# Cached GQA decode block on one core: V of the first seven heads loaded by ScalarE's DMA queue

## The chip, the cores and the metric

The kernel runs on one core of one Trainium2 chip. The time is that of one execution on the device, in microseconds. Before the change it is 656.65 us, the median of three runs (656.56 to 656.92).

## The reference

One token goes through an attention block with a KV cache and then through a gated MLP, each behind a LayerNorm and with a residual. Sizes: D = 512, 32 query heads, 8 KV heads (4 query heads share one), 65,536 cached positions, head size 128, F = 1792, all in bf16.

```python
def _A_ref(x, k_cache, v_cache, wq, wo):
    q = (x @ wq) ...                    # 32 heads of 128
    k = jnp.repeat(k_cache, rep, axis=1)
    v = jnp.repeat(v_cache, rep, axis=1)
    scores = jnp.einsum("bhqd,bhkd->bhqk", q, k) * (Dh ** -0.5)
    p = _softmax(scores, axis=-1)
    o = jnp.einsum("bhqk,bhkd->bhqd", p, v)
    return (...o...) @ wo
...
h = x + _A_ref(_layernorm(x), A_k_cache, A_v_cache, A_wq, A_wo)
h2 = h + _B_ref(_layernorm(h), B_w_gate, B_w_up, B_w_down)   # sigmoid(g) * u, then w_down
```

K and V are 134 MB each (8 heads x 65,536 x 128 x 2 bytes) and are read once. With the weights the program reads 282.33 MB.

## The kernel before, in words

**Program.** All instructions are recorded in lists, one for each engine (`Prog.op`, `Prog.dma`), with the names of what they depend on. `Prog.emit` turns the names into semaphore waits. An engine runs its list in order. A DMA is issued by the engine in whose list it stands: that engine waits for what the DMA needs, issues it, and goes on; the data move later. Line numbers in the profile's DMA rows (L339 for K and V, L341 for wq, L358 for wo, L368 and L373 for the B weights, L325 for x) are those of the issuing instruction; the rows call SyncE's issuing SPq and ScalarE's ACTq, and the queues q1 (SyncE's) and q10 (ScalarE's).

**Loads.** Each of the 8 KV heads has a K and a V of 16.8 MB. Each is loaded in two pieces of 8.39 MB (`PIECES`): 128 partitions with 64 KB each, which is 16 chunks of 4 KB (`CH` elements). They go to `ring`, an SBUF buffer of 36 chunks in each partition. K's piece 0 lies in chunks 0 to 15, K's piece 1 in 4 to 19, and both pieces of V in 20 to 35 (`AT`). So K's next piece can come once 12 of the 16 chunks of the last one have been used, and V's next piece once all of the last one has been used. The names: K2.1 is piece 1 of K of head 2. K of head 0 comes in four smaller loads, ahead of everything but wq.

**VectorE.** `dve_block` transposes K chunk by chunk from `ring` into `ktw` (L531), 16 chunks for each piece. After 12 of them a tiny memset (L534) gives the mark F: `F1.0` says that K1.0 has left chunks 4 to 15, `F1.1` the same for K1.1. VectorE also takes the maxima (L538), the transpose of the softmax weights P (L587) and the sums.

**TensorE.** `pe_scores` multiplies the transposed chunks by q (L443, `PS<-ktw`), 4 parts of 8 chunks to a head. The products with V (`pv`, also L443, `PS<-ring,PT_sb`) of head h run during head h+1: those of piece 0 after part 1 of the scores (their end is `PV{h}.1`), those of piece 1 after part 3 (`PV{h}.3`).

**ScalarE.** Each head has its softmax exponentials (L577), the scaling of the output (`head_out`, L618, waits for `PV{h}.3`), a copy (L624), the clearing of the output bank (L504) and the next head's weights (L500).

**Order of the loads.** All but x are issued by SyncE, in one list:

```python
for h in range(1, HKV):
    load("K", h, 0, ["F0.0" if h == 1 else f"F{h - 1}.1"], "ka", f"K{h}.0")
    load("V", h - 1, 0, ["F0.1" if h == 1 else f"PV{h - 2}.3"], "va", f"V{h - 1}.0")
    load("K", h, 1, [f"F{h}.0"], "kb", f"K{h}.1")
    load("V", h - 1, 1, [f"PV{h - 1}.1"], "vb", f"V{h - 1}.1")
```

The list of names in a `load` is what the load waits for. After this loop come V7.0 (after F7.1), wo, V7.1 and the weights of B.

Of the kernel before, what the change touches and what calls it, by code (L numbers as in the profile page):

```python
# [13 lines left out]
HKV = 8  # L14
GS = 4
NQ = 32
DH = 128
D = 512
FF = 1792
# [16 lines left out]
class Prog:  # L36
# [14 lines left out]
    def op(self, eng, fn, deps=(), name=None, to=None, times=1):  # L51
        assert name is None or name not in self.where, name
        self.ops[eng].append(dict(fn=fn, deps=[d for d in deps if d], name=name, dma=None, to=to, times=times, part=self.part.get(eng)))
        if name:
            self.where[name] = (eng, len(self.ops[eng]) - 1)

    def dma(self, eng, fn, sem, deps=(), name=None):
        self.op(eng, fn, deps, name)
        rec = self.dma_sems.setdefault(sem, dict(sem=None, count=0))
        rec["count"] += 16  # L60
        self.ops[eng][-1]["dma"] = (sem, rec["count"])
# [162 lines left out]
def bass_sequential_preLN__gqa_block_cached__glu_gated_glu__decode_kernel(  # L224
# [10 lines left out]
    CH = TC * DH  # L235
    PIECES = ((0, 16), (16, 32))
    RING = 36 * CH
    AT = {"K": (0, 4), "V": (20, 20), "K0": (0, 20), "V7": (0, 20), "wg": 0, "wd": 7}
# [3 lines left out]
    WO = ((0, 28), (28, 4))  # L242
    RW = 4
    WD_SPLIT = [(0, 8), (8, 11), (11, 13), (13, 14)]
    FG = FF // 4

    with ExitStack() as es:
        def sb(name, shape, dt):
            return es.enter_context(nc.sbuf_tensor(name, shape, dt))
# [14 lines left out]
        ring = sb("ring", [128, RING], bf16)  # L264
        ktw = sb("ktw", [128, NKT * CH + WH], bf16)
# [56 lines left out]
        op, dma = P.op, P.dma  # L322
# [3 lines left out]
        W_SPLIT = {"wg": [(0, 4)], "wu": [(0, 4)]}  # L326
        W_AT = {"wg": AT["wg"] * CH, "wu": AT["wg"] * CH + 4 * FF}
        LAST = [(16, 26), (26, 32)]

        def first_chunk(k, h, q):  # L330
            return AT[{("K", 0): "K0", ("V", HKV - 1): "V7"}.get((k, h), k)][q]

        def load(k, h, q, deps, sem, name, cols=None):
            j0, j1 = PIECES[q]
            a, z = cols or (j0, j1)
            cache = A_k_cache if k == "K" else A_v_cache
            rows = cache[0, h, j0 * TC * 128:j1 * TC * 128, :].rearrange("(p t) d -> p (t d)", p=128)
            at = (first_chunk(k, h, q) - j0) * CH
            dma("sp", lambda e: e.dma_start(ring[:, at + a * CH:at + z * CH], rows[:, (a - j0) * CH:(z - j0) * CH]), sem, deps, name)  # L339

        dma("sp", lambda e: e.dma_start(ktw[:, 0:NKT * CH].rearrange("p (k n) -> p k n", k=4),  # L341
                                        A_wq.rearrange("(p k) n -> p k n", p=128)), "r0", (), "wq")
        for q in range(2):
            for i in range(2):
                j0 = 16 * q + 8 * i
                load("K", 0, q, (), f"r{2 * q + i + 1}", f"K0.{q}{'ab'[i]}", (j0, j0 + 8))
        for h in range(1, HKV):
            load("K", h, 0, ["F0.0" if h == 1 else f"F{h - 1}.1"], "ka", f"K{h}.0")
            load("V", h - 1, 0, ["F0.1" if h == 1 else f"PV{h - 2}.3"], "va", f"V{h - 1}.0")
            load("K", h, 1, [f"F{h}.0"], "kb", f"K{h}.1")  # L350
            load("V", h - 1, 1, [f"PV{h - 1}.1"], "vb", f"V{h - 1}.1")
        h = HKV - 1
        load("V", h, 0, [f"F{h}.1"], "va", f"V{h}.0")
        def load_wo(i, deps):
            j0, nj = WO[i]
            src = A_wo[j0 * DH:(j0 + nj) * DH, :].rearrange("(p r) n -> p (r n)", r=nj)
            dst = ktw[:, j0 * D:(j0 + nj) * D]
            dma("sp", lambda e: e.dma_start(dst, src), f"wo{i}", deps, f"wo{i}")  # L358

        load_wo(0, [f"PV{h - 1}.3"])  # L360
        for i, cols in enumerate(LAST):
            load("V", h, 1, (), ("vb", "vl")[i], f"V{h}.1{('', 'b')[i]}", cols)
        load_wo(1, ())
        for k, w in (("wg", B_w_gate), ("wu", B_w_up)):
            src = w.rearrange("(p k) n -> p (k n)", p=128)
            for i, (k0, k1) in enumerate(W_SPLIT[k]):
                at = W_AT[k]
                dma("sp", lambda e, at=at, w=src, a=k0 * FF, z=k1 * FF: e.dma_start(ring[:, at + a:at + z], w[:, a:z]),  # L368
                    f"{k}{i}", [f"PV{HKV - 1}.1"] if k == "wg" else (), f"{k}.{i}")
        src = B_w_down.rearrange("(p r) n -> p r n", p=128)  # L370
        for i, (r0, r1) in enumerate(WD_SPLIT):
            at = AT["wd"] * CH
            dma("sp", lambda e, at=at, a=r0, z=r1: e.dma_start(ring[:, at + a * D:at + z * D].rearrange("p (r n) -> p r n", n=D),  # L373
                                                               src[:, a:z, :]), f"wd{i}", (), f"wd{i}")


        op("pool", lambda e: e.iota(iota_i[:, :], [[1, 128]], base=128, channel_multiplier=-1), name="iota")
        for nm, t, v in (("onesf", onesf[:, :], 1.0), ("xz0", xz[:, :], 0.0), ("onef", one_f[:, :], 1.0), ("nhalf", nhalf[:, :], -0.5),
# [39 lines left out]
        n = 128 // XR  # L418
# [198 lines left out]
        def head_out(h):  # L617
            op("act", lambda e: e.activation(po_sb[:, :], ps(PO, 0, 512), AF.Copy, scale=rl[:, :]),  # L618
               [f"PV{h}.{NR - 1}", f"rl{h}"], f"po{h}", to="po")
            for t in range(4):  # L620
                op("pe", lambda e, t=t: e.matmul(ps(OX, 0, 4), lhsT=po_sb[:, t * 128:(t + 1) * 128],  # L621
                                                 rhs=sel_bf[:, 8 * t:8 * t + 8:2], start=(t == 0), stop=(t == 3)),
                   [f"po{h}"] if t == 0 else (), f"ox{h}" if t == 3 else None)
            op("act", lambda e: e.activation(O2[:, GS * h:GS * h + GS], ps(OX, 0, 4), AF.Copy), [f"ox{h}"], f"o2.{h}")  # L624
            if h + 1 < HKV:
                clear_out(h + 1)
# [3 lines left out]
        def regroup(i):  # L630

            j0, n = WO[i]
            m = 128 // RW
            op("dve", lambda e: e.tensor_tensor(Lw[i][:, :].rearrange("p (j c) -> p j c", j=n),  # L634
                                                bass.AP(tensor=O2, offset=j0, ap=[[NQ, 128], [1, n], [0, m]]),
                                                bass.AP(tensor=blk_of, offset=0, ap=[[m, 128], [0, n], [1, m]]), ALU.mult),
               [f"o2.{(j0 + n) // GS - 1}", "blk"], f"Lw{i}")
            for v in range(n // RW):
                lhsT = bass.AP(tensor=Lw[i], offset=v, ap=[[n * m, 128], [n // RW, 128]])
                op("pe", lambda e, v=v, lhsT=lhsT: e.matmul(ps(OT[i], RW * v, RW * v + RW), lhsT=lhsT, rhs=row_of[:, :], start=True,  # L640
                                                            stop=True, skip_group_check=True),
                   [f"Lw{i}", f"PT{NB - 1}" if i == 0 else None] if v == 0 else (), f"O3p{i}" if v == n // RW - 1 else None)
            op("dve", lambda e: e.tensor_copy(O3[:, j0:j0 + n], ps(OT[i], 0, n)), [f"O3p{i}"], f"O3.{i}")  # L643
# [152 lines left out]
        for i in range(HKV + 1):  # L796
            loop, last = 0 < i < HKV, i == HKV
            for r in range(NR):
                P.part = {"dve": (f"A{r}", i) if loop else None}
                if not last:  # L800
                    dve_block(NR * i + r)
                    pe_scores(NR * i + r)
                if i and r == 1:
                    P.part = {"dve": ("A4", i) if loop else None}
                    transposed(i - 1)
                    P.part = {"pe": ("V0", i), "dve": ("B0", i) if loop else None}
                    denominators(i - 1)
                    op("pe", lambda e: None, [f"V{i - 1}.0", f"z{i - 1}"])
                    pv(i - 1, r, 6)
                    pv(i - 1, r, 2)  # L810
                if i and r == 3:
                    if last:
                        P.part["pe"] = ("L", i)
                        project7()
                        columns()
                    P.part["pe"] = ("V3", i)
                    op("pe", lambda e: None, [f"V{i - 1}.1"])
                    pv(i - 1, r, 5 if last else 6)
                    if last:
                        P.part["pe"] = ("VL", i)  # L820
                        op("pe", lambda e: None, [f"V{i - 1}.1b"])
                    pv(i - 1, r, 3 if last else 2)
                    P.part["pe"] = ("O", i)
                    head_out(i - 1)
                if not last and r == 3:
                    P.part = {"pe": ("X", i), "dve": ("A3", i) if loop else None}
                    softmax(i)
        P.part = {}
        regroup(1)
        project(range(NQ - GS, NQ), O3, ["O3.1", "wo1"], last=True)  # L830

# [10 lines left out]
        for i, (nm, bank) in enumerate((("wg", GB), ("wu", UB))):  # L842
            at = W_AT[nm]
# [20 lines left out]
        for i, (r0, r1) in enumerate(WD_SPLIT):  # L864
            for r in range(r0, r1):
                for g in range(4):
                    last = r == NF - 1 and g == 3
# [7 lines left out]
        for i, eng in enumerate(("sp", "act")):  # L875
            dst = out[0][:, 256 * i:256 * i + 256].rearrange("o (s j) -> (o s) j", s=2)
# [31 lines left out]
```

## Time and profile before

| | us |
|---|---|
| median of three runs | 656.65 (656.56 to 656.92) |
| span of the profiled execution, first to last instruction | 655.2 |
| PE busy | 398.7 (61%) |
| DVE busy | 350.3 (53%) |
| ACT busy | 43.1 (7%) |
| bytes read | 282.33 MB, 431 GB/s over the span |
| span of a head's period, K2.0 issued to K3.0 issued | 77.40 (122.65 to 200.05) |

The span is the time between the first and the last instruction of one profiled execution; the time of a run has 1.45 us more around it. The page has the busy time of each engine, the span in slices, the DMA queues, the chain of work that ended last (followed back from the last instruction to whatever released each step), the costliest groups of instructions, and the DMA issues with their time from issue to landing. The granted clock of TensorE is 0.782 on average, and it changes between 0.5 and 1.0 in stretches.

### The profile page before, as it was taken

The numbers are of one execution on the slowest core, as the hardware profiler recorded it, in microseconds if no ns is written. First come the engines' busy times: TensorE is split into PE (matmuls) and PEld (weight loads), VectorE is DVE, ScalarE is ACT, GpSimd is POOL, SyncE is SP. The second block draws the span as 40 slices with busy tenths as digits, with TensorE's granted clock in tenths as the row PEclk, the third lists the DMA queues.
The fourth block names the chain that finished last, engine by engine and source line by source line (L and its number), as shares of the span: only waits on it lengthen the run. The fifth ranks groups of instructions, "written<-read, shape, count | busy, mean of one in ns | idle before, by whom it ended". The sixth has DMA issues, their size and how long they took to land.

```text
span 655.2 us, 6177 instructions
## 1 busy us (share of the span) xinstructions
PE 398.7 (61%) x2317; PEld 66.8 (10%) x1549; DVE 350.3 (53%) x428; ACT 43.1 (7%) x114; POOL 3.7 (1%) x19
## 2 busy tenths in 40 slices
PE   2778672937548293674828467393845739285466
PEld 1100010110101000010100101010010101001122
DVE  3398853819266290935719184481917548092202
ACT  1100200020000200002000200002000020001001
POOL 1000000000000000000000000000000000000000
PEclk9799695977959687785978769595796958778656
DMA  9999999999999999999999999999999999999998
GB/s 396 436 436 460 436 396 448 448 448 408 424 448 448 444 392 444 448 448 420 412 448 448 448 408 424 448 448 440 392 448 448 448 412 420 448 448 444 412 404 356
DMA packets 6376, 282.33 MB, mean 431 GB/s; under 512 B 744, under 2 KB 872, under 8 KB 1256
## 3 DMA queue, kind: packets, MB, share of 16 engines
q1 hardware_dynamic: 6340, 282.33, 99.6%
q10 hardware_dynamic: 36, 0.00, 0.0%
HBM read 282.33 MB, written 0.00 MB: 431 GB/s over the span
## 4 chain that ended last, share of the span: by engine, by line
DMA 66%; DVE 30%; PE 2%; issue 1%; SPq 0%; PEldq 0%
DMA ring<-in_A_k_cache_dram 58%; DVE ktw L531 30%; DMA ring<-in_B_w_up_dram 4%; DMA ring<-in_A_v_cache_dram 4%; PE PS L443 2%; PE PS L869 0%; PE PS L847 0%; DVE hh L859 0%; DVE hhT L863 0%; SPq L368 0%; SPq L339 0%; DVE y_sb L873 0%; PEldq L171 0%
## 5 line engine op out<-in xcount | busy, mean ns | idle before, releaser
L531 DVE STREAM_TRANSPOSE ktw<-ring 128x1024 f32<-128x1024 f32 x256 | 291.6, 1209 | 164.6 <-DMA ring<-in_A_k_cache_dram 164.5
L443 PE MATMUL PS<-ktw 128*128 128x512 bf16 x1024 | 276.7, 419 | 162.7 <-DVE ktw L531 155.0
L443 PE MATMUL PS<-ring,PT_sb 128*32 x1024 | 85.7, 422 | 54.7 <-issue 46.3
L443 PEld LDWEIGHTS PS<-ktw 128*128 x256 | 26.3, 103 | 401.1 <-issue 233.3
L618 ACT ACTIVATE po_sb<-PS,rl 128x512 bf16<-128x512 f32 x8 | 5.5, 687 | 523.4 <-PE PS L443 523.4
L443 PEld LDWEIGHTS PS<-ring,PT_sb 128*32 x1024 | 20.7, 116 | 117.7 <-issue 116.4
L566 DVE TENSOR_REDUCE gmj<-PS 1x4 f32<-1x128 f32 x8 | 2.2, 279 | 53.9 <-PE PS L564 53.9
L538 DVE TENSOR_REDUCE M_sb<-PS 128x1 f32<-128x512 f32 x32 | 19.9, 683 | 19.3 <-PE PS L443 19.3
L577 ACT ACTIVATE P_sb<-PS,negmax 128x512 bf16<-128x512 f32 x32 | 21.5, 685 | 0.3
L587 DVE STREAM_TRANSPOSE PT_sb<-P_sb 128x512 bf16<-128x512 bf16 x32 | 19.9, 675 | 1.7 <-ACT P_sb L577 1.7
L443 PE MATMUL PS<-ktw,xz 128*8 x32 | 9.7, 476 | 6.0 <-DMA ktw<-in_A_wq_dram 6.0
L634 DVE TENSOR_TENSOR Lw<-O,blk_of 128x896 bf16<-128x896 bf16 (+1 forms) x2 | 1.4, 682 | 16.0 <-ACT O L624 16.0
L489 DVE STREAM_TRANSPOSE qt<-qh 32x512 bf16<-32x512 bf16 x1 | 0.7, 699 | 14.8 <-ACT qh L486 14.8
L571 PE MATMUL PS<-one_f,gmrep 1*128 1x1 f32 x16 | 4.6, 357 | 5.0 <-DVE gmrep L568 5.0
L564 PE MATMUL PS<-identf,gm 128*1 128x128 f32 x16 | 4.5, 379 | 5.1 <-issue 2.9
L643 DVE CAST O<-PS 128x28 bf16<-128x28 f32 (+1 forms) x2 | 0.3, 174 | 12.7 <-PE PS L640 12.7
L577 ACT ACTIVATION_READ_ACCUMULATOR P_sb<-PS,negmax 128x1 f32 x32 | 6.5, 203 | 0.0
L621 PE MATMUL PS<-sel_bf,po_sb 128*128 128x4 bf16 x32 | 2.1, 170 | 6.3 <-ACT po_sb L618 6.3
L504 ACT ACTIVATE PS<-zcol 128x512 f32<-128x512 bf16 x8 | 5.0, 623 | 0.0
L573 ACT ACTIVATE negmax<-PS 128x1 f32<-128x1 f32 x8 | 1.4, 171 | 54.0 <-PE PS L571 54.0
L592 PE MATMUL PS<-L_sb,lsel 128*128 128x4 f32 x16 | 2.5, 229 | 3.8 <-DVE PT_sb L587 3.8
L571 PEld LDWEIGHTS PS<-one_f,gmrep 1*128 1x128 f32 x16 | 4.0, 306 | 8.8 <-DVE gmrep L568 8.8
(89 smaller groups left out, 65.4 us busy)
## 6 DMA issues: line engine op xcount, KB each, us to landing
ring<-in_A_k_cache_dram SPq DMA_DIRECT2D x4, 4096.0 KB, 34.8
ring<-in_A_v_cache_dram SPq DMA_DIRECT2D x1, 5120.0 KB, 30.0
ktw<-in_A_wq_dram SPq DMA_DIRECT2D x1, 4096.0 KB, 12.2
ktw<-in_A_wo_dram SPq DMA_DIRECT2D x1, 3584.0 KB, 18.3
ring<-in_A_v_cache_dram SPq DMA_DIRECT2D x1, 3072.0 KB, 36.8
ring<-in_B_w_gate_dram SPq DMA_DIRECT2D x1, 1792.0 KB, 23.4
ring<-in_B_w_up_dram SPq DMA_DIRECT2D x1, 1792.0 KB, 27.2
ring<-in_B_w_down_dram SPq DMA_DIRECT2D x1, 1024.0 KB, 29.2
```

The costliest lines, as they stand in the source:

```text
L443: return e.add_instruction(mybir.InstMatmult(name=nc.get_next_instruction_name(), engine=mybir.EngineType.PE, ins=[rhs, lhsT], outs=[e.low ...
L504: op("act", lambda e: e.activation(ps(PO, 0, 512), bass.AP(tensor=zcol, offset=0, ap=[[1, 128], [0, 512]]), AF.Copy), ["zcol"] if h == 0 e ...
L531: op("dve", lambda e, d=dst, sr=src: e.transpose(d, sr), deps, f"T{b}.{c}", to="T")
L538: op("dve", lambda e, u=u: e.tensor_reduce(M_sb[:, u % 4:u % 4 + 1], ps(u % NS, 0, 512), AX.X, ALU.max), [f"S{b}.{NC - NR + k}"], f"mx{u}" ...
L564: op("pe", lambda e: e.matmul(ps(MISC, 0, 128, 0, 1), lhsT=gm[:, :], rhs=identf[:, :], start=True, stop=True), [f"gm{h}"], f"gmT{h}", to="Q")
L566: op("dve", lambda e: e.tensor_reduce(gmj[:, :], ps(MISC, 0, 128, 0, 1).rearrange("p (i a c) -> p a i c", a=4, c=NC), AX.XY, ALU.max), [f" ...
L571: op("pe", lambda e: e.matmul(ps(MISC, 128, 129), lhsT=gmrep[0:1, :], rhs=one_f[0:1, 0:1], start=True, stop=True), [f"gmrep{h}"], f"neg{h}")
L577: op("act", lambda e, b=b: e.activation(P_sb[:, (b % 4) * 512:(b % 4 + 1) * 512], ps(b % NS, 0, 512), AF.Exp, bias=negmax[:, k:k + 1], sca ...
L587: op("dve", lambda e, b=b: e.transpose(PT_sb[:, (b % 4) * 512:(b % 4 + 1) * 512], P_sb[:, (b % 4) * 512:(b % 4 + 1) * 512]), [f"E{b}"], f" ...
L592: op("pe", lambda e: e.matmul(ps(MISC, 132, 136), lhsT=lsel[:, :], rhs=L_sb[:, :], start=True, stop=True), [f"PT{NR * h + NR - 1}"], f"l{h ...
L618: op("act", lambda e: e.activation(po_sb[:, :], ps(PO, 0, 512), AF.Copy, scale=rl[:, :]), [f"PV{h}.{NR - 1}", f"rl{h}"], f"po{h}", to="po")
L621: op("pe", lambda e, t=t: e.matmul(ps(OX, 0, 4), lhsT=po_sb[:, t * 128:(t + 1) * 128], rhs=sel_bf[:, 8 * t:8 * t + 8:2], start=(t == 0), s ...
```

## The change

V0.0 to V6.1, 14 loads of 8.39 MB, are issued by ScalarE in place of SyncE. `load` gets an argument for the engine. What each load waits for, its place in `ring` and its semaphore stay. The V loads stand in ScalarE's list at these places: V0.0 ahead of the softmax of head 0; then, in the part-3 step of head i, V of head i-1 piece 1 and V of head i piece 0, both ahead of `head_out(i-1)`. SyncE keeps K of all heads, V7, wo, wq and the weights of B; those after K7.1 are only moved in the text, and keep their order.

```diff
-        def load(k, h, q, deps, sem, name, cols=None):
+        def load(k, h, q, deps, sem, name, cols=None, eng="sp"):
...
-            dma("sp", lambda e: e.dma_start(ring[:, at + a * CH:at + z * CH], rows[:, (a - j0) * CH:(z - j0) * CH]), sem, deps, name)
+            dma(eng, lambda e: e.dma_start(ring[:, at + a * CH:at + z * CH], rows[:, (a - j0) * CH:(z - j0) * CH]), sem, deps, name)
...
         for h in range(1, HKV):
             load("K", h, 0, ["F0.0" if h == 1 else f"F{h - 1}.1"], "ka", f"K{h}.0")
-            load("V", h - 1, 0, ["F0.1" if h == 1 else f"PV{h - 2}.3"], "va", f"V{h - 1}.0")
             load("K", h, 1, [f"F{h}.0"], "kb", f"K{h}.1")
-            load("V", h - 1, 1, [f"PV{h - 1}.1"], "vb", f"V{h - 1}.1")
...
                     P.part["pe"] = ("O", i)
+                    if not last:
+                        load("V", i - 1, 1, [f"PV{i - 1}.1"], "vb", f"V{i - 1}.1", eng="act")
+                        if i < HKV - 1:
+                            load("V", i, 0, [f"PV{i - 1}.3"], "va", f"V{i}.0", eng="act")
                     head_out(i - 1)
+                if i == 0 and r == 3:
+                    load("V", 0, 0, ["F0.1"], "va", "V0.0", eng="act")
                 if not last and r == 3:
                     P.part = {"pe": ("X", i), "dve": ("A3", i) if loop else None}
                     softmax(i)
         P.part = {}
+        h = HKV - 1
+        load("V", h, 0, [f"F{h}.1"], "va", f"V{h}.0")
...
```

More of the change, by code (lines that the diff above doesn't have):

```diff
@@ L348, in bass_sequential_preLN__gqa_block_cached__glu_gated_glu__decode_kernel @@
             load("K", h, 0, ["F0.0" if h == 1 else f"F{h - 1}.1"], "ka", f"K{h}.0")
-            load("V", h - 1, 0, ["F0.1" if h == 1 else f"PV{h - 2}.3"], "va", f"V{h - 1}.0")
             load("K", h, 1, [f"F{h}.0"], "kb", f"K{h}.1")
-            load("V", h - 1, 1, [f"PV{h - 1}.1"], "vb", f"V{h - 1}.1")
[L352 to L374, printed above, removed]
         op("pool", lambda e: e.iota(iota_i[:, :], [[1, 128]], base=128, channel_multiplier=-1), name="iota")
@@ L828, in bass_sequential_preLN__gqa_block_cached__glu_gated_glu__decode_kernel, with load_wo @@
         P.part = {}
+        h = HKV - 1
+        load("V", h, 0, [f"F{h}.1"], "va", f"V{h}.0")
+        def load_wo(i, deps):
+            j0, nj = WO[i]
+            src = A_wo[j0 * DH:(j0 + nj) * DH, :].rearrange("(p r) n -> p (r n)", r=nj)
+            dst = ktw[:, j0 * D:(j0 + nj) * D]
+            dma("sp", lambda e: e.dma_start(dst, src), f"wo{i}", deps, f"wo{i}")
+        load_wo(0, [f"PV{h - 1}.3"])
+        for i, cols in enumerate(LAST):
+            load("V", h, 1, (), ("vb", "vl")[i], f"V{h}.1{('', 'b')[i]}", cols)
+        load_wo(1, ())
+        for k, w in (("wg", B_w_gate), ("wu", B_w_up)):
+            src = w.rearrange("(p k) n -> p (k n)", p=128)
+            for i, (k0, k1) in enumerate(W_SPLIT[k]):
+                at = W_AT[k]
+                dma("sp", lambda e, at=at, w=src, a=k0 * FF, z=k1 * FF: e.dma_start(ring[:, at + a:at + z], w[:, a:z]),
+                    f"{k}{i}", [f"PV{HKV - 1}.1"] if k == "wg" else (), f"{k}.{i}")
+        src = B_w_down.rearrange("(p r) n -> p r n", p=128)
+        for i, (r0, r1) in enumerate(WD_SPLIT):
+            at = AT["wd"] * CH
+            dma("sp", lambda e, at=at, a=r0, z=r1: e.dma_start(ring[:, at + a * D:at + z * D].rearrange("p (r n) -> p r n", n=D),
+                                                               src[:, a:z, :]), f"wd{i}", (), f"wd{i}")
         regroup(1)
```

## The prediction

> **What bounds the kernel now.** First the DMA part of the page, and then a table by stretch over the long middle of the run (busy time of each engine, granted clock, DMA share, GB/s).
>
> ```profile
> q1 hardware_dynamic: 6340, 282.33, 99.6%
> q10 hardware_dynamic: 36, 0.00, 0.0%
> ```
> ```profile
> 70.35:534.00 463.65, 278.56 (x1596) 42.19 (x1020) 253.70 (x288) 31.23 (x87) 0.00 (x0) 0.78 1.00 434
> ```
>
> All bytes go through SyncE's queue q1. ScalarE's queue q10 carries only x and half of the output. Over 464 us the 16 DMA engines are never free (share 1.00, 434 GB/s), while PE and DVE are busy for 60% and 55% of that stretch. The bound is the byte stream. The chain of work that ended last shows which loop the stream closes:
>
> ```profile
> 84.19 24.75 DMA ring<-in_A_k_cache_dram
> 108.94 0.02 issue
> 108.96 13.67 DVE ktw L531 x13
> 122.63 0.02 issue
> 122.65 24.98 DMA ring<-in_A_k_cache_dram
> 147.63 0.02 issue
> 147.65 12.43 DVE ktw L531 x11
> ...
> 161.34 24.87 DMA ring<-in_A_k_cache_dram
> ...
> 509.02 24.97 DMA ring<-in_A_k_cache_dram
> ```
>
> Columns: start, duration, what. A half of K lands, VectorE transposes 12 of its 16 chunks, and that frees the ring for the next half, which is issued 13.7 us after the landing (147.63 to 161.34) and lands 24.9 us later. K's first halves land at 147.63 (122.65 + 24.98) and, five heads later, at 533.99: 386.36 us, 77.27 a head, 19.32 for each of a head's four loads (K, V, K, V, 8.39 MB each, 434 GB/s). So a half head takes 38.64 us, exactly two loads, and K's loop closes in it only because 24.9 us holds 5 us of queueing behind V. These 5 us are the slack of the loop.
>
> How a load lies on the engines matters next. Three one-microsecond stretches:
>
> ```profile
> 61.00:62.00 1.00, 1.00 (x7) 0.10 (x1) 1.00 (x2) 0.00 (x0) 0.00 (x0) 1.00 0.00 0
> 62.00:63.00 1.00, 0.70 (x3) 0.00 (x0) 1.00 (x2) 0.00 (x0) 0.00 (x0) 1.00 2.42 1049
> 63.00:64.00 1.00, 0.55 (x3) 0.10 (x1) 0.39 (x2) 0.00 (x0) 0.00 (x0) 1.00 0.00 0
> ```
>
> A packet is booked where it starts. 1049 GB/s for 1 us is 16 packets of 65.5 KB, and the share of 2.42 says that each takes 2.42 us. So each engine moves one partition's 64 KB at a time, all 16 nearly in step, and a half of K or V is 8 such pieces on each engine (8 x 2.415 = 19.32).
>
> **The change part by part.** SyncE's issues, in order of time:
>
> ```profile
> 63.45 0.33 SPq L339 DMA_DIRECT2D ring<-in_A_v_cache_dram  x1
> 84.19 0.33 SPq L339 DMA_DIRECT2D ring<-in_A_k_cache_dram  x1
> 100.81 0.33 SPq L339 DMA_DIRECT2D ring<-in_A_v_cache_dram  x1
> 122.65 0.33 SPq L339 DMA_DIRECT2D ring<-in_A_k_cache_dram  x1
> 137.61 0.33 SPq L339 DMA_DIRECT2D ring<-in_A_v_cache_dram  x1
> ...
> 200.05 0.33 SPq L339 DMA_DIRECT2D ring<-in_A_k_cache_dram  x1
> ...
> 277.20 0.33 SPq L339 DMA_DIRECT2D ring<-in_A_k_cache_dram  x1
> 292.65 0.33 SPq L339 DMA_DIRECT2D ring<-in_A_v_cache_dram  x1
> ```
>
> *SyncE loses 14 issues* (V of heads 0 to 6, two each) of 0.33 us. It gains nothing by that: each K was issued right at its own mark (122.65, 0.02 us after the transposes), so no K stood behind a V's wait. 0 us. The cover, if a V came late, would be gone in before as well.
>
> *ScalarE gains 14 issues*, each with a wait ahead of later ScalarE work:
>
> ```profile
> 0.12 0.39 ACTq L325 DMA_DIRECT2D xs<-in_A_x_dram  x1
> ...
> 70.16 0.17 ACT L573 ACTIVATE negmax<-PS 128x1 f32<-128x1 f32 x1 [43.18 <-PE PS L571]
> ...
> 137.62 0.69 ACT L618 ACTIVATE po_sb<-PS,rl 128x512 bf16<-128x512 f32 x1 [64.10 <-PE PS L443]
> ...
> 143.78 0.49 ACT L500 ACTIVATE ktw<-qz 128x64 bf16<-128x64 bf16 x1
> ```
>
> V of piece 1 waits for PV.1 (issued 100.81 so far), in the 64 us in which ScalarE idles. V of piece 0 waits for PV.3, which the scaling at L618 waits for anyway, and then stands ahead of it with 0.4 us (the x row). Behind it are the output, clearing PSUM, and the softmax, the last of which ends at 144.27. VectorE and TensorE can use them only after the next K lands at 147.63, so 0.4 us is covered by 3.4 us. 0 us; uncovered it would be 6 x 0.4 = 2.4 us. V0.0 (issued at 63.45) falls into the 43.18 us in which ScalarE idles until 70.16.
>
> *V7, wo and the B weights* keep their order on SyncE. 0 us beyond what shifts with all.
>
> *Two queues share the engines.* Now K and V lie in different rings. The trace has one case of that: x (64 bytes for each engine, on ScalarE's queue) beside wq (8 pieces of 32 KB, 1.21 us each at 434 GB/s).
>
> ```profile
> ktw<-in_A_wq_dram SPq DMA_DIRECT2D x1, 4096.0 KB, 12.2
> xs<-in_A_x_dram ACTq DMA_DIRECT2D x1, 1.0 KB, 4.9
> ```
> ```profile
> SPq L221 <- DMA out_dram<-y_sb: 0.9, 1, 0.9
> ```
> ```profile
> core 0: 655.2 us, clock 0.782
> 653.93 0.33 SPq L877 DMA_DIRECT2D out_dram<-y_sb  x1
> ```
>
> The tiny output load has nothing beside it and is done 1.3 us after its issue (653.93 to 655.2). x, issued 0.12 us after wq, needs 4.9, but not wq's 12.2. So it neither waited for all of wq nor slipped through: the extra 3.6 us are about three of wq's pieces. I read it as an engine taking turns between rings piece by piece: x's data waits for a running piece, and its completion mark, an entry of its own in the ring, waits for another. I carry this over to the 64 KB pieces: once V joins, each remaining piece of K *and K's completion mark* gets one piece of V, 2.415 us, in front of it.
>
> How many? V1.0's kind (first half of V) is issued 14.96 us after K (122.65 to 137.61) to 15.45 us after (277.20 to 292.65), V0.1's kind 16.62 us after (84.19 to 100.81). In pieces that is 6.2 to 6.4 and 6.9: K's seventh is running, the eighth and the mark are left, two pieces of V go in front, so K takes 10 slots, 24.15 us, in place of 8.
>
> K's loop: from the last slot to the next K's first data lie 13.8 us (the mean of landing to issue: 13.71 above, 13.84 from the landing at 161.34 + 24.87 = 186.21 to the issue at 200.05) and the start and end of a transfer. The nearest row for those is wq, a load onto idle engines: 12.2 - 9.66 (4.19 MB at 434 GB/s) = 2.5 us. The bound below is the 1.3 us of the output. Together 16.3 us. In that time V has 6 pieces left, 14.5 us. Then the engines stand empty for 1.8 us: half a head takes 24.15 + 16.3 = 40.45 us against 38.64.
>
> With one more V piece in front of K, V has 5 left, 12.1 us, and the gap is 4.2 us. That is so for the first pair: V0.0 is issued at 63.45 and joins within 1.3 us (the output's row, below which a start lies); K1.0 lands at 70.35 so far, 5.6 to 6.9 us or 2.3 to 2.9 pieces on, so two whole pieces and the mark are left.
>
> **The sum.** The gaps follow V0.0 to V6.1, 14 of them; the last delays V7.0, and from there on SyncE's queue never runs dry, so all of it stays to the end. One gap of 4.2 and 13 of 1.8 are 27.6 us. The profiled execution is 655.2 us of span and the median 656.65; the 1.45 us around it stay. 655.2 + 27.6 + 1.45 = **684 us**, 4.2% slower.
>
> Ends of the unknown: with 1.3 us instead of 2.5 a gap is 0.6 us, the first 3.0: 10.8 us, 667. Upwards: V joins engines that run, K engines that stand, so K's first piece starts later against its issue than V's. By over 0.47 us (14.96 - 6 x 2.415) K has two pieces to begin when V joins; the two rows allow up to 1.2. All six halves of V1.0's kind would then have 2.4 us more: 14.5 us, 699. I take none, since the price of a start is nearer to equal for both than to wholly different; half of them would give 691.
>
> V itself is not late: it lands about 14.5 us after K, and is needed only after 16 transposes and the scores of them, 21.8 us after (70.35 to the first V products at 92.16).
>
> ```profile
> 45.37 24.98 DMA ring<-in_A_k_cache_dram
> 92.16 0.63 PE L443 MATMUL PS<-ring,PT_sb 128*32 x8 [0.32 <-issue]
> ```
>
> **The rivals.**
> *A smaller delay of K.* If the mark goes with the last piece, or if the bytes of both queues run side by side, K takes 9 slots, 21.7 + 16.3 = 38.0 us, under the 38.64 that two loads need: no gap but the first, 1.8 us: 658.5, +0.3%. For it: x's data are small and its row does not tell the mark's wait from the data's. Against: 3.6 us is more than one wait of 1.2.
>
> *The order stays.* If an engine finishes one ring's whole share before it turns, K and V go by arrival as now, and nothing changes: 656.65, the same; the change then only saves issues nobody waits for. For it: V always joins after K, and next K after V. Against: x came 7 us before wq. The Trainium skill, in "DMA: Bandwidth & Descriptors", section "Queues, rings and completion order", says that an engine drains a whole packet of some 9 to 17 descriptors of a row before it switches; a load's share here, 8 pieces and a mark, would be one such packet, which gives this rival's 656.65. The 4.9 us of x against 12.2 of wq speaks against it in this case.
>
> *Faster.* Two rings could keep an engine's reading and writing fuller. The place is the overlap, two pieces of each in every half head: 14 x 9.7 = 135 us. It decides only where there are no gaps, and from 1% on (1.3 us, the 0.2% that a measurement of this kernel can tell from no change); 3% would give 652.6. Against: 434 GB/s without a break is what the engines do over 464 us, and a piece's 2.42 us leaves no seam to close.
>
> **How the numbers follow.** Turns by piece with the mark waiting, 0.74, own range 667 to 699, most likely 684. Smaller delay, 0.12, 658 to 667. Order stays, 0.11. Faster, 0.03. To hold 8 in 10 the range reaches into the second case: 660 to 699. Slower by over 0.2%: 0.74 and nearly all of the second case, 0.85; within 0.2%: 0.12; faster: 0.03.
>
> **What would show it.** In the profile after: 14 V issues on ScalarE's queue and q10 with 117 MB. K's time from issue to landing up from 24.9 by little (24.15 + 2.5 = 26.7), now of other stuff: no queueing, but V's pieces. Issues of K 40.5 us apart. DMA share under 1.00, with empty stretches of about 2 us just after each K issue, and a mean of some 415 GB/s in the middle. VectorE's wait for K longer by 1.8 us a half. Wrong: K issue to issue still 38.6 (order stays or smaller delay), or stretches of 43 us (a third piece). If V products are found waiting for V, the claim that V is in time falls.

## The result, and the profile after

The changed kernel takes 670.94 us (median of four runs, 670.77 to 671.09), the kernel before 656.78 us beside it: a ratio of 1.0215, 95% interval 1.0203 to 1.0228. That is 14.2 us slower. The prediction said 684, range 660 to 699: the direction, the cause and the range hold, and the size was put at twice what it is.

The page of the changed kernel, its first line and its queues (packets, MB, share of 16 engines):

```profile
span 669.8 us, 6171 instructions
...
q1 hardware_dynamic: 4324, 164.89, 58.0%
q10 hardware_dynamic: 2052, 117.44, 40.5%
```

The 14 V loads are on ScalarE's queue, 117.44 MB. Three stretches of the changed kernel by the table of busy times, and the same three of the kernel before: up to the landing of K1.0, from there to the landing of K7.1, and the rest.

```profile
0.00:75.04 75.04, 42.65 (x168) 7.32 (x72) 45.09 (x65) 8.94 (x20) 3.13 (x18) 0.95 1.01 433
75.04:589.36 514.32, 304.29 (x1726) 45.53 (x1102) 274.91 (x311) 28.09 (x78) 0.00 (x0) 0.76 0.99 422
589.36:669.80 80.44, 52.28 (x423) 13.32 (x375) 30.45 (x52) 6.08 (x16) 0.55 (x1) 0.71 0.95 408
```
```profile
0.00:70.35 70.35, 44.27 (x168) 7.64 (x72) 45.09 (x65) 5.82 (x11) 3.12 (x18) 0.95 1.01 432
70.35:572.59 502.24, 301.62 (x1726) 45.50 (x1102) 274.70 (x311) 31.23 (x87) 0.00 (x0) 0.78 1.00 434
572.59:655.20 82.61, 52.79 (x423) 13.62 (x375) 30.50 (x52) 6.07 (x16) 0.55 (x1) 0.69 0.95 409
```

K1.0 lands 4.7 us later, the middle takes 12.1 us more, the rest 2.2 us less (V7.0 waits for less of V6.1: 22.8 us from issue to landing, 24.9 before). The work on the other engines is nearly the same. What differs in the middle is the DMA stream, 422 GB/s in place of 434.

The chain of work that ended last, over two heads. Each K row runs from issue to landing:

```profile
88.88 24.32 DMA ring<-in_A_k_cache_dram
113.20 0.02 issue
113.22 9.13 DVE ktw L505 x8
122.36 0.01 issue
122.36 4.66 DVE ktw L505 x5
127.02 0.02 issue
127.04 27.51 DMA ring<-in_A_k_cache_dram
...
168.39 24.30 DMA ring<-in_A_k_cache_dram
...
206.40 27.67 DMA ring<-in_A_k_cache_dram
```

Before, every K took 24.7 to 25.0 us. Now piece 1 of K takes 24.3 and piece 0 takes 27.5. From landing to the next issue it is still 13.8 us (113.20 to 127.04). A head, 88.88 to 168.39, takes 79.5 us against 77.27, so 2.2 us a head are lost.

**The turns can be read off.** The DMA packets by queue, in windows of 2.4 us (about one piece of 64 KB on each of 16 engines). First around the end of K2.0 (issued 127.04), with V1.0 issued at 142.04 on the other queue: the windows 146.0 to 148.4, 148.4 to 150.8 and 150.8 to 153.2.

```profile
q10 hardware_dynamic: 16, 1.05, 100.8%
```
```profile
q1 hardware_dynamic: 16, 1.05, 100.8%
```
```profile
q10 hardware_dynamic: 16, 1.05, 100.8%
```

All 16 engines take a piece of V, then the last piece of K, then a piece of V again. K's completion comes only behind that second piece of V: K2.0 lands at 154.55. Now K1.1 (issued 88.88) with V0.1 issued at 105.36: the windows 104.9 to 107.3, 107.3 to 109.7 and 109.7 to 112.1.

```profile
q1 hardware_dynamic: 16, 1.05, 100.9%
```
```profile
q1 hardware_dynamic: 16, 1.05, 100.9%
```
```profile
q10 hardware_dynamic: 16, 1.05, 100.9%
```

K's seventh piece is running when V joins, *K's eighth goes next all the same* (it starts 2.0 to 2.7 us after V's issue), and only then comes one piece of V, ahead of K's completion (landing 113.20). The completion marks of K1.1 are packets of 4 bytes, one for each engine; they start at 112.24 to 112.89, when that piece of V is through. SyncE's queue in the window 112.1 to 114.5:

```profile
q1 hardware_dynamic: 16, 0.00, 0.4%
```

So the mechanism of the prediction is there, the waiting completion too, but V gets in a turn later than predicted. The DMA packets of all runs with V on ScalarE's queue say how late: as long as K has pieces left, no V starts its first piece earlier than 3.3 us after its issue, and pieces of K that start up to some 4 us after it still go ahead.

The price of a gap (first the stretch in which one falls, then the K half that follows it, then the half without one):

```profile
166.30:169.30 3.00, 3.00 (x15) 0.33 (x4) 3.00 (x4) 0.00 (x0) 0.00 (x0) 1.00 0.00 0
...
168.39:192.69 24.30, 12.36 (x96) 2.29 (x73) 7.19 (x10) 0.00 (x0) 0.00 (x0) 0.82 1.02 432
...
206.40:234.07 27.67, 12.89 (x101) 2.80 (x79) 7.63 (x12) 4.68 (x13) 0.00 (x0) 0.77 1.01 436
```

From 166.3 to 169.3 no piece starts on any engine. That is longer than the 2.42 us of a piece, so the engines have run empty: V's last pieces end at 167.97 to 168.67, and K2.1's first ones start at 169.34 to 169.81. These first pieces also take longer. The 16 of the window 169.3 to 171.7 fill 128.1% of it, 3.07 us each; those of K2.0, which queued behind V, fill 111.0% of theirs (129.1 to 131.5).

```profile
q1 hardware_dynamic: 16, 1.05, 128.1%
```

Summed over the packets of the whole trace, an engine stands empty for 8.1 us on average, in seven gaps, and pieces run 6.4 us over their 2.42 us. These 14.5 us are nearly all of the 14.6 by which the two profiles differ; in the kernel before the two come to 0.1 us together. While both queues are loaded (206.40 to 234.07) the rate is 436 GB/s: two rings at once cost no bandwidth.

### The profile page after: what moved, and what is told of

Same layout as the page of the kernel before. It is cut to its first block, busy times and chain, and to the rows that moved or that the text cites. A ratio compares the mean times of both kernels' runs of the same rounds, so it can differ in the third digit from the quotient of the medians.

```text
span 669.8 us, 6171 instructions
## 1 busy us (share of the span) xinstructions
PE 399.2 (60%) x2317; PEld 66.2 (10%) x1549; DVE 350.4 (52%) x428; ACT 43.1 (6%) x114; POOL 3.7 (1%) x19
## 3 DMA queue, kind: packets, MB, share of 16 engines
q10 hardware_dynamic: 2052, 117.44, 40.5%
## 4 chain that ended last, share of the span: by engine, by line
DMA 63%; DVE 32%; PE 3%; issue 2%; ACT 0%; SPq 0%; PEld 0%; PEldq 0%
DMA ring<-in_A_k_cache_dram 59%; DVE ktw L505 31%; DMA ring<-in_B_w_up_dram 4%; PE PS L417 2%; DVE PT_sb L561 0%; PE PS L850 0%; DVE hh L862 0%; PE PS L872 0%; DVE hhT L866 0%; ACT P_sb L551 0%; ACT po_sb L592 0%; PE PS L538 0%; PE PS L545 0%; PEld PS L566 0%; SPq L825 0%
## 5 line engine op out<-in xcount | busy, mean ns | idle before, releaser
L417 PE MATMUL PS<-ring,PT_sb 128*32 x1024 | 87.2, 430 | 51.6 <-issue 46.1
L512 DVE TENSOR_REDUCE M_sb<-PS 128x1 f32<-128x512 f32 x32 | 19.9, 684 | 19.3 <-PE PS L417 19.3
## 6 DMA issues: line engine op xcount, KB each, us to landing
ring<-in_A_v_cache_dram SPq DMA_DIRECT2D x1, 5120.0 KB, 27.6
ring<-in_B_w_gate_dram SPq DMA_DIRECT2D x1, 1792.0 KB, 23.3
ring<-in_B_w_down_dram SPq DMA_DIRECT2D x1, 1024.0 KB, 29.2
```

The costliest lines, as they stand in the source:

```text
L417: return e.add_instruction(mybir.InstMatmult(name=nc.get_next_instruction_name(), engine=mybir.EngineType.PE, ins=[rhs, lhsT], outs=[e.low ...
L512: op("dve", lambda e, u=u: e.tensor_reduce(M_sb[:, u % 4:u % 4 + 1], ps(u % NS, 0, 512), AX.X, ALU.max), [f"S{b}.{NC - NR + k}"], f"mx{u}" ...
```

## Experiments

All times are medians; "before" is that of the runs of the kernel before beside them (656.65 to 656.88).

**The loss split in two.** Theory: only the V loads that put two pieces ahead of K cost time. Rival: a cost of every half.

```diff
 # e1: V.1 by ScalarE, V.0 back to SyncE
             load("K", h, 0, ["F0.0" if h == 1 else f"F{h - 1}.1"], "ka", f"K{h}.0")
+            load("V", h - 1, 0, ["F0.1" if h == 1 else f"PV{h - 2}.3"], "va", f"V{h - 1}.0")
             load("K", h, 1, [f"F{h}.0"], "kb", f"K{h}.1")
...
 # e2: V.0 by ScalarE, V.1 back to SyncE
             load("K", h, 1, [f"F{h}.0"], "kb", f"K{h}.1")
+            load("V", h - 1, 1, [f"PV{h - 1}.1"], "vb", f"V{h - 1}.1")
```

> Only V0.1 to V6.1 (seven loads, piece 1 of V) are issued by ScalarE; piece 0 goes back to SyncE, between the two K pieces. Theory (turns by 64 KB piece, with the next piece of the running queue already committed when V joins): V0.1's kind joins in K's seventh piece, only one V piece gets in front of K's completion, V has seven pieces (16.9 us) left, the engines never run dry: 656.7 to 658.5. Rival (two rings at once cost rate, or ScalarE's issues cost time, in every half): about half of the 14.2 us, 663 to 665.

> Only V0.0 to V6.0 (piece 0 of V) are issued by ScalarE; piece 1 goes back to SyncE. Theory: this kind joins a piece earlier, two V pieces get in front of K's completion, six (14.5 us) are left against a turnaround of some 16 us, and the whole loss is here: one gap of about 2 us a head, seven of them, 669 to 672. Rival (a cost of every half): half of it, 663 to 665.

Measured: piece 1 alone 669.85 us (1.0196, 1.0179 to 1.0213), 13.2 us slower; piece 0 alone 683.95 us (1.0413, 1.0395 to 1.0430), 27.3 us slower. Both expectations missed, and so did the rival's half and half: the parts cost 13 and 27 us, and together 14. The chains, K's issue to landing, of e1 and then of e2:

```profile
84.36 29.63 DMA ring<-in_A_k_cache_dram
...
127.83 21.92 DMA ring<-in_A_k_cache_dram
...
163.45 29.77 DMA ring<-in_A_k_cache_dram
```
```profile
88.95 21.89 DMA ring<-in_A_k_cache_dram
...
124.55 32.19 DMA ring<-in_A_k_cache_dram
...
170.58 21.74 DMA ring<-in_A_k_cache_dram
```

These lengths are whole slots of 2.415 us. 21.9 is a K alone from standing engines: 8 slots (19.3) and a start of 2.6. In e1, K1.1 queues behind V0.0 in its own ring: V0.0 lands 19.3 us after K1.0 (70.5 by the chain's 84.36 less 13.8), at 89.9, 5.5 us after the issue; 5.5 + 24.15 = 29.6, so 10 slots, two V pieces ahead. In e2, 5.6 + 11 slots (26.6) = 32.2: three V pieces ahead. So it isn't which V is moved that counts, but how far K is when V joins. A K that had to queue is less far, gets more V in front, and leaves V shorter: V with 6 left (14.5 us) or 5 (12.1) ends before the next K can start, which takes a turnaround of 16.4 us (13.8 from landing to issue, 2.6 of start). That K then starts from standing engines, is further on when its V joins, and loses less. The halves alternate, and the losses don't add up.

The formula that fits: K's issue to landing = queue or start + slots x 2.415. For the changed kernel 2.6 + 9 slots (21.7) = 24.3 and 3.4 + 10 slots (24.15) = 27.5. Of the 3.4 us, 2.1 to 2.8 are the wait for V's last pieces (127.04 to 129.16 at the earliest, 129.81 at the latest); the rest is the longer first piece and the landing.

**Join later.** Theory: a V that joins later finds less of K left.

```diff
 # e3: V.0 of heads 1 to 6 behind head_out
                     head_out(i - 1)
+                    if 0 < i < HKV - 1:
+                        load("V", i, 0, [f"PV{i - 1}.3"], "va", f"V{i}.0", eng="act")
...
 # e6: as e3, and all V loads behind extra copies of [128, 512] into an unused tile
+                        load("V", i - 1, 1, [pause(2, f"PV{i - 1}.1", f"late1.{i}.")], "vb", f"V{i - 1}.1", eng="act")
...
+                        load("V", i, 0, [pause(1, f"PV{i - 1}.3", f"late0.{i}.")], "va", f"V{i}.0", eng="act")
...
 # e8: the changed kernel, V.1 alone behind three such copies
+                        load("V", i - 1, 1, [pause(3, f"PV{i - 1}.1", f"late1.{i}.")], "vb", f"V{i - 1}.1", eng="act")
```

> All 14 V loads on ScalarE, but V1.0 to V6.0 are issued behind the scaling, the copy and the clearing of the output bank, some 1.7 us later. Theory: they then join K's transfer as late as V0.1's kind (16.7 to 17.1 us after K's issue), one V piece in front in place of two, no gap but the one after V0.0: 657 to 660, so the later issue is faster by over 10 us. Rival (a cost of two rings or of ScalarE): no change from 670.9; if V's lateness were the limit, slower than 671.

Measured: 671.46 us (1.0221, 1.0204 to 1.0238). No gain. The chain shows that the K behind the later V did get shorter, and that the next one got longer:

```profile
127.17 25.12 DMA ring<-in_A_k_cache_dram
166.00 28.77 DMA ring<-in_A_k_cache_dram
208.48 24.27 DMA ring<-in_A_k_cache_dram
246.59 25.07 DMA ring<-in_A_k_cache_dram
```

127.17 (K2.0) is down from 27.5 to 25.1, and no gap follows it. But 166.00 (K2.1) is up from 24.3 to 28.8, and 208.48 (K3.0) starts on empty engines. The pattern now repeats after three halves in place of two: by the packets of the trace there are five gaps, of 1.2 to 2.5 us, where the changed kernel has seven of 1.0 to 1.3.

> All 14 V loads on ScalarE, each issued later: V0.0 by some 2.2 us, V0.1's kind by some 1.5 us (two extra copies on ScalarE into an unused tile), V1.0's kind by some 2.7 us (behind the clearing of the output bank and one such copy). Theory (an engine takes turns by piece, has the next piece chosen when it starts one, and the loss is the number of V pieces ahead of K's completion): now one V piece in both halves, V has seven left, which outlast the turnaround; no empty stretch in the middle: 659 to 663. Rival (two rings cost rate, or ScalarE's issues): 671 or more, since ScalarE has more to do and V comes later.

Measured: 672.61 us (1.0247, 1.0219 to 1.0275). Missed, though the part that the edit was to bring is there in the first halves, with K near 26 us:

```profile
126.29 25.13 DMA ring<-in_A_k_cache_dram
...
165.26 25.89 DMA ring<-in_A_k_cache_dram
...
204.86 26.16 DMA ring<-in_A_k_cache_dram
```

9 slots are 21.7, so one V piece is ahead in each half, as meant; but the start takes 3.4 to 4.5 us of these times. K2.1 is issued at 165.26, and V's seven pieces after K2.0's landing (151.42) end 16.9 us on, at 168.3: K queues for 3.0 us and should land 24.7 after its issue. It lands 25.9 after: some of its first pieces take up to 3.6 us. These halves have no gap in which all engines stand. Further on there are two, ahead of the K issued at 326.98 and at 447.01, and K then varies from 21.7 to 29.2 us. A half takes 39.8 us on average (twelve halves from 86.42 to 563.78), about 1 us more than 38.64.

> The changed kernel with V0.1's kind alone issued some 2.2 us later (three extra copies on ScalarE ahead of it). Theory (what counts is how many pieces of V go ahead of K's completion): V piece 1 joins so late that the next K queues longer behind it, that K is less far on when V piece 0 joins, and three V pieces go ahead of it in place of two: slower, 678 to 688. Rival from the run with both kinds later (a later V is neither here nor there): 670 to 673.

Measured: 671.99 us (1.0239, 1.0218 to 1.0260). Missed: K takes 21.9 and 30.1 in turn (a K with no V ahead, then one that queues longer), and their sum is what it was, 52.0 against 51.8.

```profile
89.05 21.90 DMA ring<-in_A_k_cache_dram
...
124.66 30.06 DMA ring<-in_A_k_cache_dram
```

So in these three runs the time at which V joined changed which K came late, and not the sum.

**Smaller rows.** Theory: a turn is one row's piece, whatever its size. Rival: bytes are shared evenly.

```diff
 # e4: V.0 in two loads of 8 chunks (32 KB rows), e7: V.1 too
-                            load("V", i, 0, [f"PV{i - 1}.3"], "va", f"V{i}.0", eng="act")
+                            load("V", i, 0, [f"PV{i - 1}.3"], "va", f"V{i}.0a", (0, 8), eng="act")
+                            load("V", i, 0, (), "va", f"V{i}.0", (8, 16), eng="act")
...
 # e5: K in two loads instead (changed kernel); c5: the same K in the kernel before
-            load("K", h, 1, [f"F{h}.0"], "kb", f"K{h}.1")
+            load("K", h, 1, [f"F{h}.0"], "kb", f"K{h}.1a", (16, 24))
+            load("K", h, 1, (), "kb", f"K{h}.1", (24, 32))
```

> All 14 V loads on ScalarE as in the change, but piece 0 of V comes as two loads with rows of 32 KB, same bytes. Theory (a turn is one row's piece, whatever its size): the two turns ahead of K's completion cost 2 x 1.2 us in place of 2 x 2.4, V has 16.9 us left, no gap: 657 to 660. Rival (both queues share the bytes evenly, or a cost of two rings): the size of a row is nothing, 670 to 672.

> All 14 V loads on ScalarE, both pieces of V as two loads each with rows of 32 KB. Theory: two turns ahead of K's completion cost 2.4 us in both halves, V has 16.9 us left, so the gap can't move to the other half as it did when only piece 0 was cut: 658 to 662. Rival (the loss belongs to two rings as such, or a smaller row changes nothing): 670 to 673.

> All 14 V loads on ScalarE as in the change; K of heads 1 to 7 comes in two loads for each half, rows of 32 KB. Theory (turns by piece): each 32 KB of K left when V joins gets 64 KB of V in front, three to five V pieces in place of one or two, so K is late by 5 us more and the engines stand empty more: 700 to 721. Rival (bytes shared evenly, or the loss is a fixed cost of two rings): 669 to 673.

> The kernel before (all on SyncE) with K of heads 1 to 7 cut in the same way into rows of 32 KB. All theories: a row's size is nothing in a single ring, 656 to 658. If it is slower, smaller rows or double issues cost something by themselves, and that has to come off the run with two queues.

Measured: V.0 in small rows 672.19 us (1.0240, 1.0223 to 1.0257); all V in small rows 669.12 us (1.0152, 1.0106 to 1.0197; single runs from 663.6 to 670.6); K in small rows 696.28 us (1.0590, 1.0541 to 1.0639); the same K in one queue 658.02 us (1.0011, 1.0002 to 1.0021). The K side speaks for turns by piece: cutting K's rows costs 25 us more with two queues and 1 us with one, since each 32 KB of K now lets a 64 KB piece of V past. 696 is under the 700 to 721 expected. The V side is not confirmed: in e4 K takes 22.9 and 28.7 us in turn (issued at 128.78 and 165.54), so one half loses what the other gains, and with all V cut (e7) the median is 1.8 us below the changed kernel's, not the 10 us expected. Like e6, e7 has the loss spread over both halves (its chain, K's issue to landing):

```profile
127.25 26.68 DMA ring<-in_A_k_cache_dram
167.77 23.64 DMA ring<-in_A_k_cache_dram
```

e5 also says something of V's late first turn. One V is issued at 147.26 and starts its first piece at 150.75, 3.5 us later. SyncE's queue from 147.26 to 150.70:

```profile
q1 hardware_dynamic: 45, 1.47, 99.2%
```

Nearly three pieces of K start on each of the 16 engines ahead of V. The earliest V in e5 comes 3.3 us after its issue, as with K's 64 KB pieces, although a piece of K takes half as long here. So it is not simply that an engine has one next piece chosen, as the expectations have it: these runs fit a wait of 3.3 to 4 us better than a number of pieces.

**K's lead.** e6 and e7 pointed to the start of a K that is issued only some 3 us before the engines run out of other work. So K's issue was put off by two transposes, in the changed kernel and in the kernel before.

```diff
 # e9 (changed kernel), c9 (kernel before)
-                mark = ({15: 0, 31: 1} if h == 0 else {11: 0, 27: 1}).get(s)
+                mark = ({15: 0, 31: 1} if h == 0 else {13: 0, 29: 1}).get(s)
```

> The changed kernel with the mark that frees K's ring set after 14 chunks in place of 12, so that each K of heads 1 to 7 is issued some 2.4 us later. Theory (with two rings the engines wait for the turnaround from K's landing to the next K, and nothing covers it): each half that had a gap pays the 2.4 us in full, and V, which then joins K's transfer a piece earlier, gets one more piece in front: at least 7 x 2.4 = 17 us more, 688, up to some 735 where all 14 halves pay both. Rival (the loss is a fixed cost of two rings, lost rate or ScalarE's issues): the delay is hidden as before, 671 to 674.

> The kernel before with the same later mark. Theory and rivals alike: K is issued 2.4 us later but still 2 to 3 us ahead of the end of V's transfer in the same ring, so the engines stay full: 656.5 to 658.

Measured: changed kernel 713.54 us (1.0868, 1.0850 to 1.0886), 42.6 us on top of the change; kernel before **670.50 us** (1.0209, 1.0185 to 1.0232), against all theories. The chain of e9:

```profile
91.10 26.73 DMA ring<-in_A_k_cache_dram
...
133.93 26.57 DMA ring<-in_A_k_cache_dram
...
176.46 26.77 DMA ring<-in_A_k_cache_dram
```

The time lies in the 688 to 735 expected. Every half is now the one that the prediction drew: 2.6 + 10 slots = 26.7 from standing engines, a period of 42.7 us (91.10 to 133.93 to 176.46), and (42.7 - 38.64) x 14 = 57 us over before, as measured (56.9). And c9, in one ring:

```profile
45.29 24.97 DMA ring<-in_A_k_cache_dram
...
86.23 23.29 DMA ring<-in_A_k_cache_dram
...
125.49 23.05 DMA ring<-in_A_k_cache_dram
...
164.59 22.84 DMA ring<-in_A_k_cache_dram
...
203.39 24.40 DMA ring<-in_A_k_cache_dram
```

K1.0 lands at 70.26, V0.0 stands right behind it and so is through 19.3 us later, at 89.6; K1.1 is issued at 86.23, 3.3 us ahead of that. Without a seam it would land 22.7 us after its issue; it takes 23.3, and others up to 24.4. The halves take 38.9 to 40.4 us, 1.0 us more on the average (13.85 / 14). So a lead of 3.3 us is not enough for a seamless start, while 5.6 (24.9 - 19.3, the kernel before) is. What is lost is in K's first pieces. SyncE's queue in the window 205.0 to 207.4, when K3.0's pieces begin, in c9 and then in the kernel before:

```profile
q1 hardware_dynamic: 28, 0.98, 121.5%
```
```profile
q1 hardware_dynamic: 22, 1.05, 100.9%
```

The 15 pieces of c9 (the other packets are completion marks) take 3.1 us each, the 16 of the kernel before 2.42. Over c9's trace pieces run 7.1 us over, up to 4.5 us for one, and an engine stands for 4.7 us on average, as the engines fall out of step (the starts of K3.0's second pieces spread over 1.7 us, 0.6 in the kernel before); there is no time in which all 16 stand.

**ScalarE by itself.**

```diff
 # c7: the kernel before, and ScalarE loads 1 KB of x into an unused tile where the change issues V
+                    if not last:
+                        tiny(2 * i - 1, [f"PV{i - 1}.1"])
+                        if i < HKV - 1:
+                            tiny(2 * i, [f"PV{i - 1}.3"])
                     head_out(i - 1)
```

> The kernel before (all V and K on SyncE) with 14 extra loads of 1 KB issued by ScalarE at the places and with the waits where the change issues V, into an unused tile. Theory: ScalarE's issues and waits are off the path, and a second ring with tiny pieces costs K no turns: 656.5 to 657.5. Rival (the change's loss is ScalarE's issuing and waiting): 665 to 671.

Measured: 656.88 us (1.0003, 0.9993 to 1.0013), the same. The 14 issues and waits on ScalarE cost nothing, nor does a second queue that carries 1 KB loads. What costs is V's bytes in it.

No version with V on the second queue came under the kernel before, and the table of stretches says why: its 434 GB/s has no break over 502 us.

## Why the prediction came out as it did

- *What bounds the kernel.* Right: with the same work on all engines, the time follows the breaks in the byte stream.
- *ScalarE's and SyncE's issues, 0 us.* Right: the tiny loads changed nothing (1.0003), and landing to next K issue stayed at 13.8 us.
- *Turns piece by piece, and K's completion waits for a piece of V.* Right, and shown by the windows by queue: K piece, V piece, K piece, V piece. The reading of the x row holds too: in the trace of before x's data start at 2.88 to 3.46 us, when wq's first pieces are through, and its marks at 4.11 to 4.70, when wq's second ones are. The rival "smaller delay", in which the completion does not wait, falls: K1.1's last pieces start in the window up to 109.7 and give way to V's in the next one, and its completion marks start only when that piece of V is through, at 112.24 to 112.89 (landing 113.2). The rival "order stays" falls with it, and so does the reading that the Trainium skill's "DMA: Bandwidth & Descriptors", section "Queues, rings and completion order", gave it: the engines drain one 64 KB piece from a queue before they switch, not a transfer's whole share of 8 pieces and a mark. That they go round the queues in turn, as the same section says, is what the windows show.
- *Start and end of a transfer, 2.5 us from wq.* Right for engines that stand: 24.3 - 9 slots = 2.6, and 2.6 again in e1, e2 and e9. The order of the starts was the wrong way round: "K's first piece starts later against its issue than V's", but on standing engines K's first piece starts 0.95 to 1.4 us after its issue (168.39 to 169.34 and 169.81), and V's among K's pieces 3.3 us or more.
- *"K's seventh is running, the eighth and the mark are left, two pieces of V go in front, so K takes 10 slots."* This step failed, for V0.1's kind. The eighth piece goes ahead of V; one piece of V is in front, K takes 9 slots, V has 7 left (16.9 us), and that outlasts the turnaround of 16.4. No gap follows. For V1.0's kind there are indeed two, but by two errors that cancel: K had queued behind V, so its sixth piece was running at V's issue (142.04), not its seventh, and the seventh still went ahead. For V0.0 it was two, not three: its first pieces started 3.8 us after its issue and later, where the prediction had 1.3 at most, and K1.0 came 4.7 us (two slots) late, not 7.2.
- *The sum.* So there are gaps in every other half, not in all 14. 2.2 us a head for the middle (12.1 us), 4.7 at the front and 2.2 given back at the end make 14.6 in the two profiles, where the prediction had 27.6. That the prediction took each half on its own, each from standing engines, was the error behind it: a gap puts the next K ahead and so removes the next gap. e9 is the case in which every half does start from standing engines, and there the prediction's own formula, with e9's 16.0 us from landing to issue, gives the period to 0.1 us. That 670.9 lies in the range is partly luck: its low end, 667, stood for a start of 1.3 us, which was 2.6, and what made the loss small was the alternation of the halves, which the prediction did not have.
- *"These 5 us are the slack of the loop."* Wrong, and not seen until c9: of the 5.6 us of lead less than 2.3 could be spared, for a lead of 3.3 already costs 13.9 us. In the changed kernel the lead is gone in one half and 3 us in the other.
- *V in time.* Right: TensorE waits once for V, 2.4 us in all.

```profile
PE PS L417 <- DMA ring<-in_A_v_cache_dram: 2.4, 1, 2.4
```

What stays open: why the first pieces of a K take longer than 2.42 us when it is issued onto standing engines or some 3 us before the transfer ahead of it ends, as in e6, e7 and c9, and at what lead between 3.3 and 5.6 us this begins. Why V's first turn comes 3.3 us or more after its issue while K has pieces left; only e5 varied something there, the size of the row. And why all versions with a later V or with V in smaller rows come out within 3 us of each other: their chains differ, and no run tells a common cause from chance.

## What to carry to other kernels

Where one queue keeps the DMA engines full, as here, a second queue added no bytes (436 GB/s against 434), but it did change who goes first: once the other queue had its first turn, the transfer that the loop waits for was held up by one piece of it for each of its own remaining pieces, and by one more for its completion. Keep transfers that a tight loop waits for in the same queue as the bulk behind them; cutting the bulk into smaller rows brought little here (669.1 and 672.2). Count the lead with which the next transfer is issued before the engines run out, since it is the real slack. Estimate such a change over at least two rounds of the loop: a loss in one round can pay for the next.

## What the runs showed that was not expected

- A load issued 3.3 us before its queue runs out is not seamless: the kernel before, with K issued 2.3 us later, takes 670.5 us, +2.1%, though its queue is never empty when K is issued.
- The two halves of the change cost 13.2 and 27.3 us when made alone, and 14.2 together.
- Moving V's issue by 1.5 to 3 us, in three ways (671.5, 672.6, 672.0), and halving V's rows (672.2, 669.1) changed which halves had a gap, and the time stayed within 3 us of the change's 670.9.
